# Reordering the joins of seven partial products on GpSimd, and one attention sum on VectorE, in a fused attention + MLP kernel

## The chip, the core and the metric

One Trainium2 chip, one of its cores. The metric is the device time of one execution in microseconds (us). The kernel before: median 1112.72 us of 3 runs (1112.7 to 1113.13).

## What is computed

The input is a 2048 x 576 matrix `x`. With `xn = layernorm(x)` the output is `x + A(xn) + B(xn)`:

```python
xn = _layernorm(x, axis=-1)
return x + _A_ref(xn, A_wqkv, A_wo) + _B_ref(xn, B_w1, B_b1, B_w2)
# A: 32 heads of 18; each position attends to itself and 7 earlier ones, 2 apart, then @ wo
# B: h = xn @ w1 + b1 (576 -> 4608); act = h * tanh(softplus(h)) (Mish); act @ w2 (4608 -> 576)
```

Everything is float32. The kernel splits each operand of a matrix product into a high part (a cast to fp32r) and a low part (operand minus high part), and adds three matmuls per product for it.

## The kernel before, in words

The 2048 rows are worked in two halves of 1024. For each half the kernel computes q, k, v (`qkv_item`), then the MLP in 18 steps of 256 hidden columns; behind the second half comes the output projection `wo` (`wo_part`). The attention itself never touches TensorE (PE): GpSimd (POOL) multiplies queries with windows of keys (`pr`, line 539) and weights with values (`pv`, line 577), VectorE (DVE) sums these products (lines 544 and 583) and ScalarE (ACT) takes the exponentials. This work runs beside the MLP, one piece per slot.

**Slots.** The order of all work is written out by hand. `plan` is a list of slots; each holds one piece of PE work (`add`), and `before(i, fn)` puts other work into slot `i` in front of the piece. Each engine then executes its own instructions strictly in the order in which this loop emits them. So a number in a `before` call decides what stands behind what on an engine's queue.

**The second half's MLP.** For its first 8 hidden steps the second product (`act @ w2`) is done by a scheme of seven products in place of eight (Strassen-like), `p_item` at line 861: `P7, P4, P1, P5, P2, P6, P3` in this order, for `e` = 0 to 3, each into its own accumulator `pacc[name, pr]` (two tiles of 128 x 576, `pr` = 0 and 1). Slot `("p","x",e,k)` is product `k` of round `e`. A product is 24 matmuls into four PSUM tiles `po` (line 872; the tag "out" has 4 buffers), and DVE adds each to the accumulator (line 878; ACT copies for P1, P6 and P7 in round 0, line 876). PE can begin the next user of a `po` buffer only once that addition is done.

**The joins.** When all rounds are done, `p_join(a, b, pr)` (line 880) adds one accumulator to another on POOL. There are seven for each `pr`: P6+=P1, P7+=P6, P6+=P5, P2+=P1, P3+=P6, P4+=P7, P5+=P7. The results P2, P3, P4, P5 are the four quarters of the output; `m2_cols` (line 884) then adds the remaining hidden steps to them: 24 matmuls a slot (line 893), four DVE additions (line 896), the slot for `pr` = 0 or 1 of the rows `b` = 1 first, into P4 and P5, later `b` = 0 into P2 and P3.

**Names and lines that the steps below touch.** `a_split` (lines 834, 835): ACT casts the high part of `act`, POOL subtracts for the low part. `u_high`, `u_low` (820, 826): the same for the operands of the seven products, the low part on POOL or DVE. `mish` (725, 726, 731, 732): DVE adds two PSUM parts, ACT takes Mish, ACT and POOL split. `take` (714): ACT copies a PSUM tile. Lines 680 and 686 are the matmuls of the MLP's first product, `h`.

**Where an attention sum stands.** `attention` issues a product on POOL and leaves its sum on DVE (line 544) to be flushed with the next piece. A set `behind_adds` holds slots in which the sum is emitted behind the slot's piece (and so behind its four additions on DVE); elsewhere it stands in front of them.

Of the kernel before, what the change touches and what calls it, by code (L numbers as in the profile page):

```python
# [31 lines left out]
OC = 4  # L32
# [7 lines left out]
def block_kernel(ctx: ExitStack, tc: tile.TileContext, x, wq, wo, w1, b1, w2, mask, out):  # L40
# [469 lines left out]
    behind_adds, behind_next, now = set(), set(), [0]  # L510
# [318 lines left out]
    def a_split(b, j):  # L829
        q = 2 * OC  # L830
        t = rawact[q, b, j]
        assert owner[where[q, b, j]] == (q, b, j) and (q, f"A{b + 1}{j + 1}") in held_
        a = acts[1, q, b, j] = sb.tile([P, 2, TB], F32R, tag=f"a{b}", bufs=(3, 2)[b], name=f"act_1_{b}_{2 * q + j}")
        nc.scalar.copy(a[:, 0, :], t)
        nc.gpsimd.tensor_tensor(out=a[:, 1, :], in0=t, in1=a[:, 0, :].bitcast(F32), op=ALU.subtract)
# [44 lines left out]
    def p_join(a, b, pr):  # L880
        nc.gpsimd.tensor_tensor(out=pacc[a, pr], in0=pacc[a, pr], in1=pacc[b, pr], op=ALU.add)
# [274 lines left out]
    at = {}  # L1156
# [7 lines left out]
    def before(i, fn):  # L1164
        plan[max(i, 0)][1].append(fn)
# [17 lines left out]
    items = []  # L1183
# [172 lines left out]
    def spot(hf, q, i):  # L1356
        return at["s", hf, q, i]

    for q in range(NP):
        if q == 0:  # L1360
            i = at["q", 0, 3, 1, 0]
            ps_ = dict(raw=i - 3, sums=i - 1, wa=i, wc=i + 1, t0=i + 2, t1=i + 4)
        elif q == 1:
            i = at["q", 0, 3, 0, 0]
# [16 lines left out]
    for q in range(1, 2 * OC + 1):  # L1381
        i = spot(0, q, (3,2)[q > 1])
# [5 lines left out]
    i = spot(0, NP - 1, 0)  # L1388
# [5 lines left out]
    i = at["q", 1, 0, 1, 1]  # L1394
# [4 lines left out]
    i = spot(0, 9, 4)  # L1399
# [10 lines left out]
    for q in range(NP):  # L1410
        if q == 0:
            i = at["z", JB - 1, 0]
            ps_ = dict(wa=i - 7, t0=i - 6, t1=i - 5, wc=i - 4)
        elif q == 1:
            i = spot(1, 0, 0)
# [22 lines left out]
    J = 2 * OC + 1  # L1438
    for b in range(NB):
        for j in range(2):  # L1440
            before(spot(1, J, 0) + (2,3,1,2)[2 * b + j], lambda b=b, j=j: a_split(b, j))
    for n, (a, b) in enumerate((("P6", "P1"), ("P7", "P6"), ("P6", "P5"), ("P2", "P1"), ("P3", "P6"), ("P4", "P7"), ("P5", "P7"))):
        for pr in range(2):
            i = items[-2][2] + 1 + (0,1,2)[n] if n < 3 else at["p", 1, J + 0 - 1, n > 4, pr] + (1, 7, 1, 2)[n - 3]
            before(i, lambda a=a, b=b, pr=pr: p_join(a, b, pr))

    i = at["q", 0, 1, 1, 0]
# [3 lines left out]
    i = at["q", 0, 3, 1, 0]  # L1451
# [5 lines left out]
    i = at["q", 1, 0, 1, 1]  # L1457
# [9 lines left out]
    for n in range(0, JB, 2):  # L1467
        i = at["q", 0, 1, 0, n]
# [4 lines left out]
    for n in range(TJ):  # L1473
        i = spot(0, 2 + n, 2)
# [3 lines left out]
    i = spot(0, NP - 2, 0)  # L1478
# [7 lines left out]
    for n, (name, pr) in enumerate((name, pr) for name in ("P4", "P5", "P2", "P3") for pr in range(2)):  # L1486
        i = items[dict(P4=0, P5=2, P3=2, P2=3)[name]][2] + pr
# [2 lines left out]


    att = {}
    behind_adds.update((at["p", "x", OC - 1, 4], at["p", "x", 0, 4]))
    behind_next.add(at["m", 1, 10, 3])
    T = [0.0]
    for p_ in plan:
# [37 lines left out]
    i = spot(1, *(11,3))  # L1534
# [11 lines left out]
    i = spot(1, NP - 1, 0)  # L1546
# [26 lines left out]
    last = {}  # L1573
# [44 lines left out]
```

## Time and profile before

| What | Value |
|---|---|
| Median of the runs shown | 1112.72 us |
| The profiled execution's own time | 1113.35 us |
| Its span, first to last instruction | 1111.6 us |
| PE busy | 1101.6 us, 99% of the span |
| DVE, POOL, ACT busy | 850.2, 789.8, 498.9 us |
| Granted TensorE clock | 1.000 |

The profile counts an engine as busy while an instruction of it is under way. A row of a timeline gives start, length, engine, line, operation and tiles, the number of merged instructions, and in brackets the idle time of that engine ahead of the row with what ended it. Merged rows overlap a little, as matmuls are pipelined: the distance between two rows' starts is the better measure of what a group costs. 1.75 us of the profiled execution lie outside its span (1113.35 - 1111.6).

### The profile page before, as it was taken

To read this page: it belongs to the slowest core of one execution; us is meant where nothing else is said; L and a number is where in the kernel's file an instruction comes from. 1 tells how busy PE (TensorE), PEld (TensorE's weight loads), DVE (VectorE), ACT (ScalarE), POOL (GpSimd) and SP (SyncE) were. 2 spreads that over 40 slices of the span, in tenths; PEclk is the share of its full clock that TensorE was granted. 3 is DMA by queue.
4 is the path that set the end of the run, shared out by engine and by line. 5 is a ranking of instruction groups with operands and counts; after the bars stand their busy time and mean duration, and the time that the engine had idled before them with its cause. 6 is when DMAs were issued, how large, how long until landed. Compare 5 with 4: busy or idle time off the path is not lost.

```text
span 1111.6 us, 18209 instructions
## 1 busy us (share of the span) xinstructions
PE 1101.6 (99%) x6550; PEld 1014.5 (91%) x6550; DVE 850.2 (76%) x1367; ACT 498.9 (45%) x917; POOL 789.8 (71%) x639
## 2 busy tenths in 40 slices
PE   8999999999999999999999999999999999999998
PEld 7999899999999999999999888999888999999998
DVE  6359788888889888897656567877876677777786
ACT  5544655544454544555333354443432344343353
POOL 2479777766779688685788666666688976867542
PEclk9999999999999999999999999999999999999999
DMA  6899696868777768675598799656674657776674
GB/s 200 284 311 312 231 346 225 282 237 274 255 247 263 264 212 298 249 255 201 187 322 268 225 378 304 214 189 207 219 230 161 210 195 214 245 284 219 183 233 142
DMA packets 178270, 271.60 MB, mean 244 GB/s; under 512 B 53218, under 2 KB 120068, under 8 KB 178180
## 3 DMA queue, kind: packets, MB, share of 16 engines
q1 hardware_dynamic: 178180, 270.44, 72.3%
q8 instruction: 52, 0.85, 0.3%
q14 instruction: 38, 0.31, 0.1%
HBM read 160.39 MB, written 110.00 MB: 243 GB/s over the span
## 4 chain that ended last, share of the span: by engine, by line
PE 90%; DMA 4%; DVE 2%; POOL 1%; ACT 1%; SPq 1%; issue 1%; POOLq 0%; DVEq 0%
PE h L680 27%; PE po L780 21%; PE pq L348 11%; PE po L893 11%; PE po L872 6%; PE h L686 5%; PE o L1076 5%; PE z L446 3%; DMA acc<-in_x 1%; DMA kv<-kv_d 1%; DMA t<-kept_t 1%; DMA accP<-in_x 1%; SPq L612 1%; POOL act L732 1%; DMA pw<-kept_T 1%
## 5 line engine op out<-in xcount | busy, mean ns | idle before, releaser
L780 PEld LDWEIGHTS po<-w,act 128*128 128x128 f32 x1728 | 236.4, 188 | 6.0 <-POOL act L732 0.4
L780 PE MATMUL po<-w,act 128*128 128x288 f32 x1728 | 240.7, 295 | 0.1
L539 POOL TENSOR_TENSOR pr<-q,kv 128x576 f32<-128x576 f32 x128 | 197.3, 1566 | 8.1 <-DMA q<-q_d 4.9
L732 POOL TENSOR_TENSOR act<-c,act 128x512 fp32r<-128x512 f32 x81 | 107.4, 1327 | 128.5 <-ACT act L731 127.9
L577 POOL TENSOR_TENSOR pv<-L,kv 128x576 f32<-128x576 f32 x128 | 178.4, 1488 | 24.8 <-DVE L L570 19.9
L784 DVE TENSOR_TENSOR acc<-po,acc 128x288 f32<-128x288 f32 x288 | 119.5, 449 | 29.9 <-PE po L780 28.8
L348 PE MATMUL pq<-wq,xt 128*128 128x432 f32 x672 | 136.4, 361 | 1.1 <-ACT xt L81 1.1
L893 PEld LDWEIGHTS po<-w,act 128*128 128x128 f32 x960 | 130.9, 188 | 5.9 <-DVE accP L896 3.0
L893 PE MATMUL po<-w,act 128*128 128x288 f32 x960 | 133.3, 295 | 2.4 <-DVE accP L896 2.4
L348 PEld LDWEIGHTS pq<-wq,xt 128*128 128x128 f32 x672 | 125.0, 188 | 8.1 <-ACT xt L81 1.9
L726 ACT ACTIVATE c<-c,b1c 128x512 f32<-128x512 f32 x81 | 58.7, 725 | 140.9 <-DVE c L725 140.6
L680 PE MATMUL h<-xt,t 128*128 128x512 f32 x432 | 110.6, 391 | 0.7 <-DVE rt L725 0.7
L680 PE MATMUL h<-S,t 128*128 128x512 f32 x432 | 110.5, 391 | 0.0
L583 DVE TENSOR_REDUCE og<-pv 128x144 f32<-128x1152 f32 x64 | 85.9, 1345 | 23.9 <-POOL pv L577 23.8
L680 PE MATMUL h<-xt,wa 128*128 128x512 f32 x432 | 104.1, 390 | 0.0
L544 DVE TENSOR_REDUCE L<-pr 128x64 f32<-128x1152 f32 x64 | 85.8, 1342 | 23.3 <-POOL pr L539 23.2
L714 ACT COPY c<-h 128x512 f32<-128x512 f32 x81 | 47.4, 586 | 124.5 <-PE h L686 73.4
L680 PEld LDWEIGHTS h<-xt,wa 128*128 128x128 f32 x432 | 80.9, 188 | 17.0
L872 PEld LDWEIGHTS po<-pw,u 128*128 128x128 f32 x672 | 91.9, 188 | 3.8 <-DVE accP L878 1.3
L872 PE MATMUL po<-pw,u 128*128 128x288 f32 x672 | 94.1, 295 | 0.5 <-DVE accP L878 0.3
L680 PEld LDWEIGHTS h<-xt,t 128*128 128x128 f32 x432 | 79.1, 188 | 15.6 <-DVE rt L725 1.2
L896 DVE TENSOR_TENSOR accP<-po,accP 128x288 f32<-128x288 f32 x160 | 69.0, 452 | 31.7 <-PE po L893 29.0
(228 smaller groups left out, 1852.1 us busy)
## 6 DMA issues: line engine op xcount, KB each, us to landing
kv<-kv_d SPq DMA_DIRECT2D x64, 396.0 KB, 4.8
kept_t<-t SPq DMA_DIRECT2D x36, 512.0 KB, 4.8
t<-kept_t SPq DMA_DIRECT2D x36, 512.0 KB, 6.4
rw<-in_w SPq DMA_DIRECT2D x36, 320.0 KB, 4.8
kept_wa<-wa SPq DMA_DIRECT2D x18, 640.0 KB, 4.9
kept_w<-w SPq DMA_DIRECT2D x20, 576.0 KB, 4.2
wa<-kept_wa SPq DMA_DIRECT2D x18, 640.0 KB, 5.2
w<-kept_w SPq DMA_DIRECT2D x20, 576.0 KB, 4.1
```

The source lines that it names most:

```text
L348: nc.tensor.matmul(pq[:, 0:432], XT[:, xi, tok], wt[wi][:, hl, 0:432], start=i == 0, stop=i == len(seq) - 1)
L539: nc.gpsimd.tensor_tensor(out=pr[:, x:x + hh], in0=q[:, j0 + x:j0 + x + hh, None, :].to_broadcast([P, hh, W, CU]), in1=win(kt, 0, CU, j0 + ...
L544: nc.vector.tensor_reduce(L[:, k, j0:j0 + hj].rearrange("p j w h -> p (j w h)"), pr.rearrange("p j w (h d) -> p (j w h) d", h=2), axis=AX, ...
L577: nc.gpsimd.tensor_tensor(out=pr[:, x:x + hj].rearrange("p j d w -> p j w d"), in0=L[:, k, x:x + hj, :, h:h + 1].to_broadcast([P, hj, W, DH]),
L583: nc.vector.tensor_reduce(og[:, c0:c0 + DH, :].rearrange("p d j -> p j d"), pr, axis=AX, op=ALU.add)
L680: nc.tensor.matmul(ph, wt[:, wl, wk * P:(wk + 1) * P], X[:, xs, :], start=first and i == 0, stop=last and i == len(seq) - 1, skip_group_ch ...
L732: nc.gpsimd.tensor_tensor(out=a[:, 1, :], in0=t, in1=a[:, 0, :].bitcast(F32), op=ALU.subtract)
L780: nc.tensor.matmul(po, acts[hf, q, b, j][:, al, tok], done["w2", hf, 2 * q + j][:, wl, c * HC:(c + 1) * HC], start=i == 0, stop=i == 5)
L784: nc.vector.tensor_tensor(out=t, in0=po, in1=t, op=ALU.add)
L872: nc.tensor.matmul(po, units[e, k, qq][:, al, tok], w[:, qq, wl, :], start=i == 0, stop=i == 5)
L893: nc.tensor.matmul(po, acts[hf, q, b, j][:, al, tok], done["w2", hf, 2 * q + j][:, wl, c * HC:(c + 1) * HC], start=i == 0, stop=i == 5)
L896: nc.vector.tensor_tensor(out=t, in0=po, in1=t, op=ALU.add)
```

## The change

The seven joins become another seven with the same four results. P6+=P5 followed by P3+=P6 is replaced: P5 is now added to P3 itself, in the slot of the last round's P6 product (`last`), three slots before P6+=P5 stood, and P3+=P6 later brings only P6 and P1. P7+=P6 moves one slot later. P6+=P1 and the four later joins keep their slots. Apart from that, one slot leaves `behind_adds`: that of product P2 in round 0, whose attention sum now stands in front of the four additions.

```diff
-    for n, (a, b) in enumerate((("P6", "P1"), ("P7", "P6"), ("P6", "P5"), ("P2", "P1"), ("P3", "P6"), ("P4", "P7"), ("P5", "P7"))):
-        for pr in range(2):
-            i = items[-2][2] + 1 + (0,1,2)[n] if n < 3 else at["p", 1, J + 0 - 1, n > 4, pr] + (1, 7, 1, 2)[n - 3]
+    last = at["p", "x", OC - 1, 5]
+    for pr in range(2):
+        for a, b, i in (("P3", "P5", last), ("P6", "P1", last + 1), ("P7", "P6", last + 3),
+                        ("P2", "P1", at["p", 1, J - 1, 0, pr] + 1), ("P3", "P6", at["p", 1, J - 1, 0, pr] + 7),
+                        ("P4", "P7", at["p", 1, J - 1, 1, pr] + 1), ("P5", "P7", at["p", 1, J - 1, 1, pr] + 2)):
             before(i, lambda a=a, b=b, pr=pr: p_join(a, b, pr))
...
-    behind_adds.update((at["p", "x", OC - 1, 4], at["p", "x", 0, 4]))
+    behind_adds.add(at["p", "x", OC - 1, 4])
```

What moves on the engines. First POOL, at the end of the seven products (`accP6_0` is the accumulator P6 for `pr` = 0, `act_1_1_16` a low part that `m2_cols` multiplies, `pr_1_3_0_1` an attention product). Before:

```order
L835 TENSOR_TENSOR act_1_1_16_9257<-rm2_7261,act_1_1_16_9257 128x512
L881 TENSOR_TENSOR accP6_0_7863<-accP6_0_7863,accP1_0_7480 128x576
L881 TENSOR_TENSOR accP6_1_7880<-accP6_1_7880,accP1_1_7658 128x576
L835 TENSOR_TENSOR act_1_0_16_9282<-ra2_7257,act_1_0_16_9282 128x512
L835 TENSOR_TENSOR act_1_1_17_9285<-rt0_7264,act_1_1_17_9285 128x512
L881 TENSOR_TENSOR accP7_0_7529<-accP7_0_7529,accP6_0_7863 128x576
L881 TENSOR_TENSOR accP7_1_7546<-accP7_1_7546,accP6_1_7880 128x576
L539 TENSOR_TENSOR pr_1_3_0_1_9291<-q_1_6_8854,kv0_1_6_8852 128x576 x2
L732 TENSOR_TENSOR act_1_0_20_9298<-c11_1_9_9269,act_1_0_20_9298 128x512
L835 TENSOR_TENSOR act_1_0_17_9333<-rm1_7260,act_1_0_17_9333 128x512
L881 TENSOR_TENSOR accP6_0_7863<-accP6_0_7863,accP5_0_7476 128x576
L881 TENSOR_TENSOR accP6_1_7880<-accP6_1_7880,accP5_1_7477 128x576
```

The same place of the changed kernel:

```order
L881 TENSOR_TENSOR accP3_0_7478<-accP3_0_7478,accP5_0_7476 128x576
L881 TENSOR_TENSOR accP3_1_7479<-accP3_1_7479,accP5_1_7477 128x576
L835 TENSOR_TENSOR act_1_1_16_9259<-rm2_7261,act_1_1_16_9259 128x512
L881 TENSOR_TENSOR accP6_0_7863<-accP6_0_7863,accP1_0_7480 128x576
L881 TENSOR_TENSOR accP6_1_7880<-accP6_1_7880,accP1_1_7658 128x576
L835 TENSOR_TENSOR act_1_0_16_9284<-ra2_7257,act_1_0_16_9284 128x512
L835 TENSOR_TENSOR act_1_1_17_9287<-rt0_7264,act_1_1_17_9287 128x512
L539 TENSOR_TENSOR pr_1_3_0_1_9291<-q_1_6_8854,kv0_1_6_8852 128x576 x2
L732 TENSOR_TENSOR act_1_0_20_9298<-c11_1_9_9271,act_1_0_20_9298 128x512
L835 TENSOR_TENSOR act_1_0_17_9333<-rm1_7260,act_1_0_17_9333 128x512
L881 TENSOR_TENSOR accP7_0_7529<-accP7_0_7529,accP6_0_7863 128x576
L881 TENSOR_TENSOR accP7_1_7546<-accP7_1_7546,accP6_1_7880 128x576
```

The pair that reads P5 went from the end of these rows to their front, and the P7 pair from ahead of the attention product to the end: the product now has two joins fewer ahead of it since the last `act` split, and none of the twelve rows is new or gone.

Then DVE in round 0 (`accP2` is the accumulator of product P2, `L_1_1` the attention sums, `u_0_6_1` an operand's low part). Before:

```order
L814 TENSOR_TENSOR rm4_7263<-rm4_7263,rm3_7262 128x512
L878 TENSOR_TENSOR accP2_0_7472<-po_0_4_0_0_7811,accP2_0_7472 128x288
L878 TENSOR_TENSOR accP2_0_7472<-po_0_4_0_1_7819,accP2_0_7472 128x288
L878 TENSOR_TENSOR accP2_1_7473<-po_0_4_1_0_7827,accP2_1_7473 128x288
L878 TENSOR_TENSOR accP2_1_7473<-po_0_4_1_1_7835,accP2_1_7473 128x288
L544 TENSOR_REDUCE L_1_1_7745<-pr_1_1_0_0_7747 128x64
L826 TENSOR_TENSOR u_0_6_1_7846<-rm4_7263,u_0_6_1_7846 128x512
L814 TENSOR_TENSOR rm0_7259<-ra2_7257,rm0_7259 128x512
L725 TENSOR_TENSOR rt1_7265<-h3_1_3_7777,rt1_7265 128x512
```

The same place of the changed kernel:

```order
L814 TENSOR_TENSOR rm4_7263<-rm4_7263,rm3_7262 128x512
L544 TENSOR_REDUCE L_1_1_7745<-pr_1_1_0_0_7747 128x64
L878 TENSOR_TENSOR accP2_0_7472<-po_0_4_0_0_7812,accP2_0_7472 128x288
L878 TENSOR_TENSOR accP2_0_7472<-po_0_4_0_1_7820,accP2_0_7472 128x288
L878 TENSOR_TENSOR accP2_1_7473<-po_0_4_1_0_7828,accP2_1_7473 128x288
L878 TENSOR_TENSOR accP2_1_7473<-po_0_4_1_1_7836,accP2_1_7473 128x288
L826 TENSOR_TENSOR u_0_6_1_7846<-rm4_7263,u_0_6_1_7846 128x512
L814 TENSOR_TENSOR rm0_7259<-ra2_7257,rm0_7259 128x512
L725 TENSOR_TENSOR rt1_7265<-h3_1_3_7777,rt1_7265 128x512
```

The sum moved past four additions; everything from the `u` row on keeps its place. PE, ACT and the DMA queue have the same rows in the same order in both kernels.

## The prediction

> **What bounds the kernel now.** I read the page first. PE is busy for 99% of the span, so a change is worth what it takes from, or adds to, the few places where PE stands still; time saved on another engine counts only if PE waits for it.
>
> ```profile
> PE 1101.6 (99%) x6550; PEld 1014.5 (91%) x6550; DVE 850.2 (76%) x1367; ACT 498.9 (45%) x917; POOL 789.8 (71%) x639
> ```
>
> Next the list of what PE waited for from 640 us to the end (total, times, longest):
>
> ```profile
> PE po L893 <- DVE accP L896: 2.4, 2, 1.7
> PE h L680 <- DVE rt L725: 0.7, 1, 0.7
> PE po L872 <- DVE accP L878: 0.3, 1, 0.3
> ```
>
> The largest wait is on line 893, behind DVE's additions to the join's results; the two small ones are those beside the attention sum that moves. So the change touches just the places where PE is idle. Behind them PE has no gap at all (busy time of PE, PEld, DVE, ACT, POOL, then the clock, in one stretch):
>
> ```profile
> 840.00:1054.00 214.00, 214.00 (x1322) 197.41 (x1321) 157.56 (x257) 82.14 (x124) 162.22 (x124) 1.00 0.65 220
> ```
>
> PE is busy for 214.00 of 214.00 us at clock 1.00, while POOL has 52 us free and DVE 56. What PE gains before 840 it should therefore carry to the end.
>
> PE around the big wait, in order of time:
>
> ```profile
> 830.21 1.53 PE L680 MATMUL h<-S,t 128*128 128x512 f32 x6
> 831.58 0.61 PE L686 MATMUL h<-xt,wc 128*128 128x512 f32 x2
> 833.85 1.85 PE L893 MATMUL po<-w,act 128*128 128x288 f32 x12 [1.66 <-DVE accP L896]
> 836.43 1.86 PE L893 MATMUL po<-w,act 128*128 128x288 f32 x12 [0.73 <-DVE accP L896]
> 838.13 1.54 PE L680 MATMUL h<-xt,t 128*128 128x512 f32 x6
> ```
>
> There are two waits in one group of 24 matmuls. DVE explains each:
>
> ```profile
> 832.08 1.35 DVE L544 TENSOR_REDUCE L<-pr 128x64 f32<-128x1152 f32 x1 [7.11 <-POOL pr L539]
> 833.35 0.81 DVE L896 TENSOR_TENSOR accP<-po,accP 128x288 f32<-128x288 f32 x2
> 835.91 0.82 DVE L896 TENSOR_TENSOR accP<-po,accP 128x288 f32<-128x288 f32 x2 [1.75 <-POOL accP L881]
> ```
>
> DVE had nothing it could do for 7.11 us: its next instruction in order was an attention sum whose product POOL had not made. The additions that free PE's four `po` buffers stood behind it. Then the third addition, the first into P5, waited 1.75 us more for a join on POOL: P6+=P5 reads P5, so P5 may not be overwritten before. POOL itself:
>
> ```profile
> 818.92 1.29 POOL L835 TENSOR_TENSOR act<-rm,act 128x512 fp32r<-128x512 f32 x1 [3.67 <-ACT act L834]
> ...
> 825.21 1.29 POOL L835 TENSOR_TENSOR act<-rt,act 128x512 fp32r<-128x512 f32 x1 [0.52 <-ACT act L834]
> 826.46 2.83 POOL L881 TENSOR_TENSOR accP<-accP,accP 128x576 f32<-128x576 f32 x2
> 829.23 2.81 POOL L539 TENSOR_TENSOR pr<-q,kv 128x576 f32<-128x576 f32 x2
> 832.00 1.27 POOL L732 TENSOR_TENSOR act<-c,act 128x512 fp32r<-128x512 f32 x1
> 833.23 1.28 POOL L835 TENSOR_TENSOR act<-rm,act 128x512 fp32r<-128x512 f32 x1
> 834.46 2.79 POOL L881 TENSOR_TENSOR accP<-accP,accP 128x576 f32<-128x576 f32 x2
> ```
>
> From 826.46 POOL is without a gap: P7+=P6, the attention product, two low parts, P6+=P5. Just before, it stood idle for 3.67 us.
>
> **Part 1: the joins.** Nothing is added or removed, four instructions move. (a) P3+=P5 stands where the 3.67 us gap is, 815.25 to 818.92, and needs 2.8 us (two joins, as at 826.46). P5 has had its last addition by then. P3 has not: DVE's additions of the last product now wait for this join, but PE begins that product only at 821.14 (its row stands with the rivals). The join ends at about 818.1, before POOL's next work can begin at 818.92: cost nothing, hidden by the wait for ACT's cast; without that gap it would cost POOL 2.8 us, of which the 0.52 us gap at 825.21 takes back a part. (b) P7+=P6 leaves 826.46, so the attention product runs 826.46 to 829.25 and its sum on DVE starts at about 829.3 instead of 832.08. Its first addition then starts at 829.3 + 1.27 (833.35 - 832.08) = 830.6 and frees a buffer at about 831.0. (c) The wait of 1.75 us goes altogether, since P5 was read at 818. What is late next? PE's own matmuls: the four buffers are full at 830.2, where line 680 begins, line 686 follows, and the next group can start 0.46 us after 831.58 (the distance of 686 to the following group in the rows of part 2), at 832.04. A buffer is free since 831.0, so PE does not wait. Without waits the group takes 3.17 us, and the work that started at 838.13 starts at 832.04 + 3.17 = 835.21: **2.92 us earlier**. The idle rows alone give 1.66 + 0.73 = 2.39 us; the other 0.5 us are what restarting the pipeline twice costs. Those are the bounds of this term, 2.4 and 2.9, and I take the upper, as it comes from starts that are measured.
>
> (d) P7+=P6 now runs where P6+=P5 ran, behind the two low parts (1.27 and 1.28 us), which come 2.8 us earlier. POOL's queue behind it is 2.8 us earlier too, about what PE gains, so every later low part keeps its lead over PE to a tenth. P4+=P7, the first to use P7, stands behind the next attention product and nobody waits for it. SP's queue is untouched.
>
> **Part 2: the attention sum in front of its additions.** DVE and PE in round 0:
>
> ```profile
> 684.99 1.54 DVE L878 TENSOR_TENSOR accP<-po,accP 128x288 f32<-128x288 f32 x4
> 686.45 1.34 DVE L544 TENSOR_REDUCE L<-pr 128x64 f32<-128x1152 f32 x1
> 687.71 0.68 DVE L826 TENSOR_TENSOR u<-rm,u 128x512 fp32r<-128x512 f32 x1
> 688.31 0.68 DVE L814 TENSOR_TENSOR rm<-ra,rm 128x512 f32<-128x512 f32 x1
> 688.91 0.68 DVE L725 TENSOR_TENSOR rt<-h,rt 128x512 f32<-128x512 f32 x1
> ```
>
> ```profile
> 685.49 3.44 PE L872 MATMUL po<-pw,u 128*128 128x288 f32 x24 [0.30 <-DVE accP L878]
> 689.65 1.66 PE L680 MATMUL h<-xt,t 128*128 128x512 f32 x6 [0.71 <-DVE rt L725]
> 691.14 0.62 PE L686 MATMUL h<-xt,wa 128*128 128x512 f32 x2
> 691.60 3.33 PE L872 MATMUL po<-pw,u 128*128 128x288 f32 x24
> 694.77 1.53 PE L680 MATMUL h<-S,wc 128*128 128x512 f32 x6
> 696.13 0.62 PE L686 MATMUL h<-xt,wc 128*128 128x512 f32 x2
> ```
>
> PE's group of 685.49 starts when the first addition is done. The sum now goes first and takes 687.71 - 686.45 = 1.26 us of DVE, so the group starts at 686.75. It lasts 3.17 us (691.60 to 694.77) plus 0.11 for the restart (3.44 against 3.33): it ends at 690.03. PE then used to wait for DVE's line 725 until 689.65. Line 725 stands behind all five instructions in either order and ends as before, so this wait of 0.71 us swallows most of the delay: 690.03 - 689.65 = 0.38 us stay, less the restart that goes with the wait (691.14 - 689.65 = 1.49 against 1.36 from 694.77 to 696.13), so **0.25 us later**. Bounds: 0, if the wait takes all, and 1.26, if line 725 moves with it. A gain I exclude: the sum frees a POOL buffer earlier, but POOL's next instruction waited for ACT, not for it:
>
> ```profile
> 692.13 1.29 POOL L826 TENSOR_TENSOR u<-rm,u 128x512 fp32r<-128x512 f32 x1 [4.39 <-ACT u L820]
> ```
>
> **Sum.** -2.92 + 0.25 = -2.67 us. The profiled execution, 1113.35 us (span 1111.6 and 1.75 around it), would become 1110.7; it is 0.63 above the median of the runs, 1112.72, for which I say 1110.1. A measurement of this kernel tells about 0.2% from no change, 2.2 us, so the line is at 1110.5 and the forecast lies only 0.4 us beyond it.
>
> **Rivals.** *The full price of the sum.* If line 725 moves with the additions, 1.26 us stay: 1112.72 - 2.92 + 1.26 = 1111.1. For it speaks that DVE is tight there; against it that its five instructions need the same time in any order.
>
> *No price for it:* 1109.8.
>
> *The transfer holds the product.* In the chain of work that ended last these two pieces follow each other:
>
> ```profile
> 826.26 4.33 DMA kv<-kv_d
> ...
> 830.61 1.43 POOL pr L539
> ```
>
> If the load landing at 830.59 releases the product's second half, moving joins away from ahead of it does nothing, the first wait stays and only the second goes: PE starts at 833.85, does 24 matmuls in 3.28, and gets to 837.13 in place of 838.13; 1112.72 - 1.0 + 0.25 = 1112.0. Against it: the two halves start 1.38 us apart, as POOL's back-to-back halves do, and the product reads the keys of head 6, while the load of 826.26 brings values that are used later. Releasers are inferred, and here by coincidence.
>
> *The join ahead holds up DVE.* DVE's operations from SBUF to SBUF stretch next to POOL's:
>
> ```profile
> 817.42 0.65 DVE L826 TENSOR_TENSOR u<-rm,u 128x512 fp32r<-128x512 f32 x1
> 817.99 1.54 DVE L878 TENSOR_TENSOR accP<-po,accP 128x288 f32<-128x288 f32 x4
> 819.45 1.31 DVE L826 TENSOR_TENSOR u<-ra,u 128x512 fp32r<-128x512 f32 x1
> ```
>
> With POOL idle it took 0.65 us, next to POOL 1.31. P3+=P5 now lies on the first one, until 818.1, so it ends 0.7 later, and so do four additions. The second then is issued at 820.1, but it had waited for POOL's instruction of 818.92 until 820.2 in any case and ends at 820.8 as before. So I charge nothing. If it were pushed by a whole 1.3 us, to 822.1, it would be late for the third matmul of the last product, which PE begins here:
>
> ```profile
> 821.14 3.33 PE L872 MATMUL po<-pw,u 128*128 128x288 f32 x24
> ```
>
> That is less than 0.9 us: 1111.0. The Trainium skill, page "SBUF — State Buffer", section "Who interferes with whom", says that a VectorE instruction with two SBUF inputs and a GpSimd instruction that reads SBUF exclude each other, whoever issues first holding on for its whole length. By that rule it is the first L826 that blocks, as reckoned here, and the sum stays.
>
> *Slower.* The sum in front makes P2's additions hang on POOL's product in round 0. That is made from 676.21 to 679.04, 5.9 us before the sum's turn at 684.99:
>
> ```profile
> 676.21 2.83 POOL L539 TENSOR_TENSOR pr<-q,kv 128x576 f32<-128x576 f32 x2
> ```
>
> ```profile
> DMA to landing us min/median/max: 1.7/2.1/9.1
> ```
>
> POOL comes to it behind two differences that wait for loads into `accP`, whose landing times spread by 7 us. If the product is later by more than 5.9 us, each further us goes to the additions and to PE one for one. From 8.6 us on this eats the whole gain (5.9 plus 2.67), and at 11 us the kernel ends at 1112.72 - 2.67 + 5.1 = 1115.1. The spread seen does not reach that.
>
> *The change does not do what it says*, the gain being given back behind 840: POOL is the tightest there, 162 of 214 us; about 1112.5.
>
> **How the numbers follow.** Forecast 1110.1, 0.56, with its own range 1109.6 to 1110.6: 0.46 of it below 1110.5. No price 0.09 (faster). Full price 0.13, transfer 0.09, join ahead 0.05, given back 0.04, all within 0.2%, but for 0.01 slower of the last; slower by the late product 0.04. So faster 0.55, same 0.40, slower 0.05. The range reaches over the full price and the transfer, 1109.3 to 1112.1, and leaves out the late product and the gain given back.
>
> **What would show it.** Right: in the changed profile PE's wait on line 893 is gone from the list; DVE's 7.11 us ahead of line 544 is about 4.3; no DVE addition of line 896 waits for line 881; POOL's 3.67 us gap has shrunk to about 0.8; in round 0 PE's wait for line 878 is about 1.5 us and that for line 725 is gone. Wrong: a wait of about 1.7 us left on line 893 (the transfer), a wait on line 725 left beside the longer one on 878 (full price), a new wait of PE for line 826 near 821, or any gap of PE behind 840.

## The result, and the profile after

The changed kernel takes **1110.03 us** (median of 12 executions, 1109.51 to 1110.49), the kernel before 1112.97 us in the same session (12 executions): a ratio of 0.9972, 95% interval 0.9964 to 0.9981. That is 2.94 us faster; the forecast was 1110.1 us, and 2.67 us of gain. The profiled execution took 1110.25 us, its span is 1108.5 us.

The list of what PE waited for from 640 us to the end had three rows before. Now it has one (total, times, longest):

```profile
PE po L872 <- DVE accP L878: 0.9, 1, 0.9
```

The waits on line 893 are gone, and so is the one for line 725. PE around the place of the big wait:

```profile
831.40 0.62 PE L686 MATMUL h<-xt,wc 128*128 128x512 f32 x2
831.85 3.34 PE L893 MATMUL po<-w,act 128*128 128x288 f32 x24
835.03 1.53 PE L680 MATMUL h<-xt,t 128*128 128x512 f32 x6
```

From line 686 to the next line 680 PE took 838.13 - 831.58 = 6.55 us before; it takes 835.03 - 831.40 = 3.63 us now. The difference is 2.92 us. The rest of the change of the span (3.1 us, from 1111.6 to 1108.5) is that PE arrived 0.18 us earlier in this execution.

DVE and POOL at that place:

```profile
829.12 1.35 DVE L544 TENSOR_REDUCE L<-pr 128x64 f32<-128x1152 f32 x1 [4.33 <-POOL pr L539]
830.39 1.54 DVE L896 TENSOR_TENSOR accP<-po,accP 128x288 f32<-128x288 f32 x4
```

```profile
815.10 2.82 POOL L881 TENSOR_TENSOR accP<-accP,accP 128x576 f32<-128x576 f32 x2
818.72 1.30 POOL L835 TENSOR_TENSOR act<-rm,act 128x512 fp32r<-128x512 f32 x1 [0.80 <-ACT act L834]
...
826.27 2.81 POOL L539 TENSOR_TENSOR pr<-q,kv 128x576 f32<-128x576 f32 x2
...
834.32 2.85 POOL L539 TENSOR_TENSOR pr<-q,kv 128x576 f32<-128x576 f32 x2
```

The first pair of joins lies in what was a gap of 3.67 us, of which 0.80 is left. The attention product starts at 826.27, DVE's idle time ahead of its sum is 4.33 instead of 7.11 us, and the four additions follow it as one row, with no wait for a join between them. Behind that PE has no gap:

```profile
838.00:1051.00 213.00, 213.00 (x1315) 196.41 (x1314) 156.77 (x258) 82.13 (x124) 161.41 (x123) 1.00 0.65 221
```

PE in round 0, where the sum now stands in front of the additions:

```profile
684.77 0.61 PE L686 MATMUL h<-xt,wc 128*128 128x512 f32 x2
686.30 3.44 PE L872 MATMUL po<-pw,u 128*128 128x288 f32 x24 [0.92 <-DVE accP L878]
689.58 1.54 PE L680 MATMUL h<-xt,t 128*128 128x512 f32 x6
690.96 0.61 PE L686 MATMUL h<-xt,wa 128*128 128x512 f32 x2
```

### The profile page after: what moved, and what is told of

The parts are those of the page before. It is cut to its first block, busy times and chain, and to the rows that moved or that the text cites. A ratio compares the mean times of both kernels' runs of the same rounds, so it can differ in the third digit from the quotient of the medians.

```text
span 1108.5 us, 18208 instructions
## 1 busy us (share of the span) xinstructions
PE 1100.6 (99%) x6550; PEld 1014.4 (92%) x6550; DVE 851.2 (77%) x1367; ACT 499.1 (45%) x917; POOL 789.4 (71%) x639
## 4 chain that ended last, share of the span: by engine, by line
PE 94%; DMA 2%; DVE 1%; ACT 1%; POOL 1%; issue 1%; SPq 0%; DVEq 0%; POOLq 0%
PE h L680 29%; PE po L780 21%; PE po L893 11%; PE pq L348 11%; PE po L872 7%; PE h L686 6%; PE o L1076 5%; PE z L446 4%; DMA acc<-in_x 1%; DMA accP<-in_x 1%; POOL act L732 0%; PE ta L75 0%; DVE rm L814 0%; DVE og L583 0%; ACT u L820 0%
```

## The experiments

Each was compared with runs of the kernel before on the same chip; over all of these and the 12 above the kernel before has a median of 1113.06 us (97 executions). "The joins alone" below means the changed kernel's joins with the sum left behind its additions.

**The full change once more.** No edit.

> The changed kernel once more, as the measure for its parts on the same chip. Theory (joins give 2.92 us, the attention sum in front takes back 0.25): 2.7 us below the kernel before, about 1110.1. Rival (the sum in front costs its full 1.26 us and the joins give more than reckoned): the same here; only the parts tell them apart.

Measured: 1110.36 us, ratio 0.9986 (0.9973 to 0.9999). Eight of the 11 executions lie between 1109.57 and 1110.94; in the other three, 1112.64 to 1116.24, the granted clock was 0.996 to 0.998 instead of 1.000. With the 12 of the result the median of 23 executions is 1110.12.

**The joins alone**, in two kernels that are the same, in different sessions:

```diff
-    behind_adds.add(at["p", "x", OC - 1, 4])
+    behind_adds.update((at["p", "x", OC - 1, 4], at["p", "x", 0, 4]))
```

> Only the joins are changed, the attention sum stands behind its additions as before. Theory: PE's stretch from 831.6 to 838.1 is 2.92 us shorter and round 0 is as before, so 2.9 us below the kernel before and 0.25 below the full change (about 1109.9). Rival, full price of the sum: 1.3 below the full change (1108.8). Rival, the sum in front gains something: above the full change.

> The joins of the changed kernel alone, the sum where it was before: a second measurement beside the kernel with the later sum. Theory: the sum in front costs 0.25 us, so this is 0.25 us below the full change's 1110.03, at 1109.8. Rival: the sum in front costs nothing, 1110.03, or all of its 1.26 us, 1108.8.

Measured: 1109.68 us (5 executions), ratio 0.997 (0.9958 to 0.9982), and 1110.1 us (7), ratio 0.9973 (0.9962 to 0.9983); together a median of 1110.07. The joins bring all of the gain: 1113.06 - 1110.07 = 2.99 us. In the time of whole executions the sum's place makes no difference that shows: 1110.07 without it, 1110.12 with it.

**The sum alone.** The kernel before, with the same line as in the full change:

```diff
-    behind_adds.update((at["p", "x", OC - 1, 4], at["p", "x", 0, 4]))
+    behind_adds.add(at["p", "x", OC - 1, 4])
```

> Only the attention sum of round 0 goes in front of its four additions. Theory: PE's wait for line 878 there grows from 0.3 to about 1.5 us, its wait for line 725 goes, and the kernel is 0.25 us slower than before (about 1113.2), within noise. Rival, full price: 1.26 slower (1114.2), with the wait for line 725 still there. Rival, a gain: below 1112.8.

Measured: 1113.1 us (11 executions), ratio 0.9999 (0.9991 to 1.0008). The time cannot tell 0.25 us from nothing, but the traces can, once the right starting point is found. DVE's row of instructions in round 0 does not begin with PE. Followed back, it begins with POOL's second difference of line 858, which waits for a load of `x`. Of the kernel before:

```profile
673.58 1.42 POOL L858 TENSOR_TENSOR accP<-accP,accP 128x576 f32<-128x576 f32 x1 [1.49 <-DMA accP<-in_x]
```

The same difference of the sum alone, and where PE got to:

```profile
672.60 1.44 POOL L858 TENSOR_TENSOR accP<-accP,accP 128x576 f32<-128x576 f32 x1 [1.50 <-DMA accP<-in_x]
```

```profile
685.79 3.46 PE L872 MATMUL po<-pw,u 128*128 128x288 f32 x24 [0.84 <-DVE accP L878]
690.46 0.62 PE L686 MATMUL h<-xt,wa 128*128 128x512 f32 x2
```

From that difference to PE's line 686 at the end of the round, in seven profiles:

| Kernel | Second difference | PE's line 686 | Distance, us |
|---|---|---|---|
| before (sum behind) | 673.58 | 691.14 | 17.56 |
| joins alone, second (sum behind) | 673.45 | 691.03 | 17.58 |
| changed (sum in front) | 673.12 | 690.96 | 17.84 |
| changed, once more (sum in front) | 672.76 | 690.61 | 17.85 |
| sum alone (sum in front) | 672.60 | 690.46 | 17.86 |
| two sums in front, below | 672.82 | 690.65 | 17.83 |
| sum behind line 725, below | 673.26 | 690.71 | 17.45 |

The six other profiles with the sum behind its additions give 17.56 to 17.59. So the sum in front costs 17.84 - 17.57 = **0.27 us**, in four profiles out of four. The second difference starts up to 0.98 us earlier or later from one profile to the next (672.60 to 673.58), and PE follows it. Among such shifts whole times don't show 0.27.

**P3+=P5 alone.** The joins alone, with P7+=P6 back in its old slot:

```diff
-("P7", "P6", last + 3)
+("P7", "P6", last + 2)
```

> P5 is added to P3 in the slot ahead in place of P6, but P7+=P6 keeps its old slot in front of the attention product; the sum as before. Theory: the wait for a late attention product stays (PE starts its group about 1.8 us late), the second wait, for the join that reads P5, goes: 1.0 us below the kernel before (about 1112.0). Rival, the read of P5 was the whole obstacle: 2.9 below. Rival, a transfer holds the product: also 1.0 below, and no different from the full joins.

Measured: nine of 12 executions between 1111.28 and 1112.34 (their median is 1111.75), median of all 1111.85; the other three, at 1117.68 to 1118.83, had a clock of 0.997 to 0.998. Ratio 1.0002 (0.9987 to 1.0016) over all. PE:

```profile
831.54 0.61 PE L686 MATMUL h<-xt,wc 128*128 128x512 f32 x2
833.81 3.45 PE L893 MATMUL po<-w,act 128*128 128x288 f32 x24 [1.66 <-DVE accP L896]
837.10 1.54 PE L680 MATMUL h<-xt,t 128*128 128x512 f32 x6
```

The first wait stays and the second goes: 837.10 - 831.54 = 5.56 us instead of 6.55. That is 1.0 us at the place, as reckoned for the case in which the product is not made earlier; in time the nine executions are 1.3 us below the kernel before.

**P7+=P6 alone.** The kernel before, with P7+=P6 moved into the slot of P6+=P5, ahead of it:

```diff
-            i = items[-2][2] + 1 + (0,1,2)[n] if n < 3 else ...
+            i = items[-2][2] + 1 + (0,2,2)[n] if n < 3 else ...
```

> P6+=P5 and its target stay; only P7+=P6 goes one slot later, behind the attention product (and directly ahead of P6+=P5). The sum as before. Theory: the attention product and its sum come 2.8 us earlier and PE starts its group without a wait, but the addition into P5 still waits until P6+=P5 has read it, at the same time as before, so PE is held there instead: 0 us, between 0.2 faster and 0.2 slower (about 1113.0). Rival, the two waits add up: 1.9 us below the kernel before, what the full joins give less the 1.0 of the second wait.

Measured: 1114.12 us (11 executions, 1112.43 to 1116.46), ratio 1.001 (1.0001 to 1.002).

```profile
831.14 1.74 PE L893 MATMUL po<-w,act 128*128 128x288 f32 x12
835.54 2.46 PE L893 MATMUL po<-w,act 128*128 128x288 f32 x12 [2.66 <-DVE accP L896]
837.80 2.53 PE L680 MATMUL h<-xt,t 128*128 128x512 f32 x6
840.17 0.62 PE L686 MATMUL h<-xt,wa 128*128 128x512 f32 x2
```

The first wait goes, but the second takes over all of it, since P6+=P5 stands where it stood and the third addition needs it: one wait of 2.66 us in place of 1.66 and 0.73. So the two moves don't add up; either alone brings 1.0 us or nothing, both together 2.9. There is more. The matmuls behind the wait are slow: 12 of them take 2.26 us to the next row, against 838.13 - 836.43 = 1.70 before, and the six of line 680 2.37 against 1.4. The windows show why (columns as before, the clock is the third number from the end):

```profile
835.50:836.50 1.00, 0.96 (x7) 0.96 (x8) 1.00 (x3) 0.02 (x1) 1.00 (x2) 1.00 0.00 0
836.50:839.90 3.40, 3.40 (x12) 2.97 (x11) 2.24 (x5) 1.32 (x2) 3.40 (x3) 0.50 0.00 0
839.90:850.00 10.10, 10.10 (x66) 9.40 (x65) 5.48 (x11) 2.66 (x4) 10.10 (x9) 1.00 0.05 13
```

One us after PE resumed its clock was halved for 3.4 us, which costs about 1.7 us. In eight of the 11 executions the mean clock was 0.997 or 0.998, and these took 1113.65 to 1116.46 us; in the three at 1.000 they took 1112.43 to 1113.12, the time of the kernel before.

**The idle time made longer.** The kernel of the last experiment, with a third pair of joins ahead of P6+=P5 in the same slot (P7 here takes in P1 once too often, and with it the outputs P4 and P5). Against the kernel before:

```diff
-(("P6", "P1"), ("P7", "P6"), ("P6", "P5"), ("P2", "P1"), ...
+(("P6", "P1"), ("P7", "P6"), ("P7", "P1"), ("P6", "P5"), ("P2", "P1"), ...
...
-            i = items[-2][2] + 1 + (0,1,2)[n] if n < 3 else ...
+            i = items[-2][2] + 1 + (0,2,2,2)[n] if n < 4 else ...
```

> The kernel with P7+=P6 beside P6+=P5 in one slot, and a third pair of joins between them, P7+=P1, 2.8 us on POOL (P1 is added to P7 once too often, and so to the outputs P4 and P5). PE's idle time on line 893 grows from 2.66 to about 5.4 us. Theory, the clock goes down when an idle time is long enough: with 2.66 us it went down in 8 of 11 executions, with 5.4 us it goes down in all; low for about 3.4 us, which costs 1.7. Time: 1112.8 (the three executions of 2.66 us with the clock at 1.000) + 2.8 + 1.7 = 1117.3. Rival, the clock's drops have nothing to do with the length of the idle time: some executions stay at 1.000, and their time is 1115.6.

Measured: 1118.64 us (4 executions, 1118.25 to 1120.38), ratio 1.0053 (1.004 to 1.0067), and the clock at 0.997 in each of the four. PE's wait is 5.37 us. PE, then two windows of its profile:

```profile
838.90 3.25 PE L893 MATMUL po<-w,act 128*128 128x288 f32 x12 [5.37 <-DVE accP L896]
```

```profile
833.60:837.30 3.70, 0.00 (x0) 0.00 (x0) 0.00 (x0) 0.00 (x0) 3.70 (x4) 1.00 0.15 60
837.30:844.10 6.80, 5.20 (x18) 4.71 (x19) 4.32 (x8) 1.34 (x2) 6.80 (x6) 0.51 0.00 0
```

The clock is low for 6.8 us, twice the 3.4 of before, and PE works in 5.2 of them, which costs 2.6 us rather than the 1.7 expected: 1112.8 + 2.7 + 2.6 = 1118.1, half a us below the measured time. The theory's direction stands, the length of the low stretch was mis-sized.

**The same slot, the pairs swapped.** P7+=P6 in the slot of P6+=P5 again, but behind it (P7 takes in P5 as well, and so do P4 and P5). Against the kernel before:

```diff
-(("P6", "P1"), ("P7", "P6"), ("P6", "P5"), ("P2", "P1"), ...
+(("P6", "P1"), ("P6", "P5"), ("P7", "P6"), ("P2", "P1"), ...
...
-            i = items[-2][2] + 1 + (0,1,2)[n] if n < 3 else ...
+            i = items[-2][2] + 1 + (0,2,2)[n] if n < 3 else ...
```

> The kernel with P7+=P6 beside P6+=P5 in one slot, but with the two pairs swapped: P6+=P5 comes first. (P7 takes in P5 as well here, and so do the outputs P4 and P5.) Theory: what held PE for 2.66 us was only that P6+=P5 stood behind two other joins on POOL. First in the slot, its half for tile 0 ends at about 832.2, and DVE's third addition is wanted at 832.9: PE's waits on line 893 are gone, the clock stays at 1.000 in all executions, and the time is that of the full change, about 1110.1. Rival: any join after the attention product makes the additions wait, whichever comes first; then 1.3 us or more of the wait stay: 1111.5 to 1114.

Measured: 1112.4 us (10 executions, 1111.71 to 1113.77), ratio 0.9994 (0.9985 to 1.0003). The theory was half right. The wait at 832 is gone and the clock is 1.000 in all ten, but most of the gain is given back a little later (in time 0.6 us of it is left):

```profile
831.79 3.54 PE L893 MATMUL po<-w,act 128*128 128x288 f32 x24
835.18 1.53 PE L680 MATMUL h<-xt,t 128*128 128x512 f32 x6
...
841.55 0.61 PE L686 MATMUL h<-xt,wc 128*128 128x512 f32 x2
842.30 3.44 PE L893 MATMUL po<-w,act 128*128 128x288 f32 x24
...
850.76 3.18 PE L893 MATMUL po<-w,act 128*128 128x288 f32 x22 [0.19 <-POOL act L732]
...
856.03 3.44 PE L893 MATMUL po<-w,act 128*128 128x288 f32 x24 [0.71 <-DVE accP L896]
```

```profile
837.04 2.86 POOL L539 TENSOR_TENSOR pr<-q,kv 128x576 f32<-128x576 f32 x2
```

Two pairs of joins stand ahead of it, from 831.49 on (four instructions, 5.63 us), and so POOL's next product starts at 837.04 instead of 834.32, 2.7 us later than in the changed kernel, while PE is as early. PE is then held up three times between 841 and 856: the group of 842.30 starts 0.75 us behind line 686 instead of 0.45, and the rows of 850.76 and 856.03 name POOL's low part and DVE's additions as what they waited for. By line 680 behind the group of 866.31 it is 869.48 - 867.35 = 2.1 us behind the changed kernel, though it left 835 only 0.15 us later. So the order alone does not bring the gain; a pair of joins has to leave this stretch, as it does in the change for the gap at 815.

**Without the gap.** The joins alone, with P3+=P5 one slot later, where POOL has no gap:

```diff
-("P3", "P5", last)
+("P3", "P5", last + 1)
```

> The joins as changed, but P3+=P5 one slot later, behind the first low part, so that POOL's idle time ahead of it no longer covers it. The sum as before. Theory: POOL's queue is 2.8 us longer where it counts; the low part act of line 835 comes late for PE by about 1.1 us and the attention product by 2.4, so PE's group starts 1.4 us later than with the full joins: 1.5 us below the kernel before. Rival, the gap is of no importance as long as P5 is read early: 2.9 below.

Measured: 1111.63 us (11 executions, 1110.71 to 1112.58), ratio 0.9989 (0.998 to 0.9998): 1.6 us above the joins alone.

```profile
818.49 1.30 POOL L835 TENSOR_TENSOR act<-rm,act 128x512 fp32r<-128x512 f32 x1 [3.58 <-ACT act L834]
819.74 6.06 POOL L881 TENSOR_TENSOR accP<-accP,accP 128x576 f32<-128x576 f32 x4
```

```profile
828.32 2.79 PE L893 MATMUL po<-w,act 128*128 128x288 f32 x19 [0.88 <-POOL act L835]
```

The gap of 3.6 us stands empty again, and P3+=P5, now the first two of four joins in a row, holds up the low part of line 835 that follows them (from 825.76; 823.20 in the changed kernel), for which PE waits 0.88 us. The gap is what makes P3+=P5 free.

**Two sums in front.** The changed kernel without the last slot of `behind_adds`:

```diff
-    behind_adds.add(at["p", "x", OC - 1, 4])
```

> The full change, and the attention sum beside product P2 of the last round goes in front of its additions as well. Theory: DVE's additions come 1.26 us later, the first is done 0.8 us after PE wants its buffer, and here no later wait of PE takes this up: 0.9 us above the full change (1110.9). Rival, DVE's idle 4.3 us a little later take it up: as the full change (1110.0). Rival, the whole of the sum's time: 1.3 above.

Measured: 1110.98 us (11 executions, 1110.48 to 1111.55), ratio 0.9981 (0.9972 to 0.9989): 0.9 us above the changed kernel. Round 3, DVE and PE:

```profile
813.45 1.34 DVE L583 TENSOR_REDUCE og<-pv 128x144 f32<-128x1152 f32 x1
814.72 1.53 DVE L878 TENSOR_TENSOR accP<-po,accP 128x288 f32<-128x288 f32 x4
```

```profile
815.26 3.41 PE L872 MATMUL po<-pw,u 128*128 128x288 f32 x24 [0.76 <-ACT u L820]
```

The additions start 1.3 us later, behind the sum, and the group waits 0.76 us plus its restart. Nothing behind swallows it, as line 725 does in round 0. The trace names ACT's cast as the releaser, because that ended last, at 815.20. In the changed kernel the same cast ended at 815.45, when the group had been running for 0.9 us, so the first matmuls don't need it; the `po` buffers are left.

**The sum later still.** The joins alone, with the sum of round 0 behind line 725:

```diff
-                    plan[now[0] + 1][0].append(behind[0])
+                    plan[now[0] + 1 + (now[0] == at["p", "x", 0, 4])][0].append(behind[0])
...
-    behind_next.add(at["m", 1, 10, 3])
+    behind_next.update((at["m", 1, 10, 3], at["p", "x", 0, 4]))
```

> All joins of the changed kernel, and the sum of round 0's P2 slot later still: behind DVE's addition of line 725 for which PE waited 0.71 us when the sum stood behind the four additions. Theory: line 725 ends 1.26 us earlier, so PE's next matmuls of line 680 follow the group of 24 without a wait: 0.71 us of wait and 0.13 to 0.2 of restart are won, the wait for line 878 stays as short as with the sum behind (0.3 to 0.4). Time 0.85 us below the joins alone: about 1108.9. Rival: DVE makes up nothing, because line 826 and the next sum behind it come later for somebody; then as the joins alone, 1109.7, with a new wait of PE near 691 to 695 us.

Measured: 1109.99 us (8 executions, 1109.6 to 1110.75), ratio 0.9973 (0.9963 to 0.9984): as the joins alone, 1110.07. The time is the rival's, but no new wait of PE appears; the mechanism is neither's. DVE, first in the second kernel of the joins alone, then here:

```profile
686.34 1.33 DVE L544 TENSOR_REDUCE L<-pr 128x64 f32<-128x1152 f32 x1
687.60 0.68 DVE L826 TENSOR_TENSOR u<-rm,u 128x512 fp32r<-128x512 f32 x1
688.80 0.68 DVE L725 TENSOR_TENSOR rt<-h,rt 128x512 f32<-128x512 f32 x1
```

```profile
686.16 1.83 DVE L826 TENSOR_TENSOR u<-rm,u 128x512 fp32r<-128x512 f32 x1
688.51 0.68 DVE L725 TENSOR_TENSOR rt<-h,rt 128x512 f32<-128x512 f32 x1
```

Line 826 takes 1.83 us instead of 0.68. POOL's product beside it ends at 687.43, and 0.56 us later the subtraction is done:

```profile
684.18 3.25 POOL L539 TENSOR_TENSOR pr<-q,kv 128x576 f32<-128x576 f32 x2
```

The sum had stood in the time in which POOL's product would have stretched that subtraction. Taken away, it won 1.26 us and lost 1.15. The Trainium skill, page "SBUF — State Buffer", section "Who interferes with whom", has the port pair that DVE's second input and GpSimd share as an exclusive lock; the subtraction has two inputs in SBUF, the sum has one and kept its 1.33 beside the same product, so the rows agree with it.

**The load earlier.** The last three experiments left the load of `x` as what starts round 0. The joins alone, with the loads into P3 one slot earlier:

```diff
-        before(i - (1 if name == "P3" else 2), lambda name=name, pr=pr: x_send(name, pr))
+        before(i - (2 if name == "P3" else 2), lambda name=name, pr=pr: x_send(name, pr))
```

> The changed kernel's joins, the sum where it was before, and the two loads of x into P3 issued one slot earlier: the second one then stands ahead of a load of 512 KB and one of 288 KB in the DMA queue. Theory: round 0 is late because POOL's second difference of line 858 waits about 1.5 us for that load (1.49 us in the profiles of the kernel before and of the joins alone); at some 390 GB/s the 800 KB less ahead of it bring it in 2.05 us earlier, so this wait goes, DVE's chain up to line 725 comes 1.49 us earlier, and PE's waits of 0.3 us for line 878 and of 0.7 us for line 725 vanish with their restarts. PE reaches the end of round 0 1.5 us earlier, and the time is 1108.6 against 1110.07 for the joins alone. Rival: PE's place there is set by its own matmuls or by the loads pushed back by 288 KB, 0.74 us each; then the time stays at 1110 or is up to 0.7 us above, and a new wait of PE or of a cast appears between 668 and 690 us.

Measured: **1108.85 us** (5 executions, 1108.51 to 1109.18), ratio 0.9959 (0.9945 to 0.9973), which is 1.2 us under the joins alone and the changed kernel. These ran in other sessions; against the kernel before in its own session, 1113.39 us there, this kernel gains 4.54 us, 1.55 more than the joins alone. POOL and PE:

```profile
670.42 2.86 POOL L858 TENSOR_TENSOR accP<-accP,accP 128x576 f32<-128x576 f32 x2
```

```profile
684.43 0.62 PE L686 MATMUL h<-xt,wc 128*128 128x512 f32 x2
684.88 3.33 PE L872 MATMUL po<-pw,u 128*128 128x288 f32 x24
688.05 1.54 PE L680 MATMUL h<-xt,t 128*128 128x512 f32 x6
689.43 0.61 PE L686 MATMUL h<-xt,wa 128*128 128x512 f32 x2
```

The two differences follow each other without a wait, PE goes from row to row, and from 640 to 1060 us its list of waits is empty. From 684.43 to 689.43 PE took 5.00 us; before it took 691.14 - 684.57 = 6.57. The profile shows 1.57 us where 1.49 was expected, the times 1.2 to 1.55.

## Why the prediction was right

**The joins.** The term was -2.92 us, between 2.4 and 2.9. The profile after shows 2.92 at the place, the joins alone 2.99 in time. The steps behind it hold one by one: the product without two joins ahead of it (826.27 instead of 829.23), the sum's wait of 4.33 us, no wait for a join, and PE's own matmuls as what is late next. The upper bound was the right one to take, since a wait costs the restart too, not only its idle row. That both moves are needed was shown by doing each alone: 1.0 us and nothing.

**The time.** That 1110.03 us lies within 0.1 us of the forecast is in part luck. The forecast was taken off 1112.72 us, the median of three executions, and the kernel before took 1112.97 in the session of the result. The gain was forecast as 2.67 and measured as 2.94 us, with an interval of 2.1 to 4.0, so the 0.3 us between them cannot be told from noise. The two terms hold by the traces, not by the time.

**That POOL's queue behind is earlier as well** was one sentence of the prediction, and it turned out to carry 2.1 us. Swapping the pairs took the wait away just as well, but left POOL as late as in the kernel before, and PE caught up with it. The rival "the gain is given back" therefore has a mechanism in this kernel; the change escapes it because a pair of joins moves into the gap. Its cover was tested too: without the gap, 1.6 us are lost.

**The sum in front.** The term was +0.25 us, and the traces show 0.27, measured from the instruction that starts the row. Full price (1.26) and a gain are excluded; in the time alone it would have stayed unsettled. But one number of this step failed: PE's wait for line 878 was said to become about 1.5 us, and it was 0.92, 1.30, 0.84 and 0.76 in the four profiles with the sum in front. The prediction took the distance between PE and DVE in round 0 from one execution as fixed. DVE's row hangs on the landing of a load, and the difference behind that load moves by up to 0.98 us between profiles, while what is late last, line 725, moves with it. The price didn't depend on that, the wait did.

**The rivals.** The transfer does not hold the product: it starts at 826.27 and its sum follows it at 829.12. The join ahead does stretch DVE's first subtraction, and it costs nothing, as reckoned, since the second would have waited for POOL anyway. The rows of the changed kernel:

```profile
817.29 1.18 DVE L826 TENSOR_TENSOR u<-rm,u 128x512 fp32r<-128x512 f32 x1
819.85 0.71 DVE L826 TENSOR_TENSOR u<-ra,u 128x512 fp32r<-128x512 f32 x1
```

1.18 and 0.71 us in place of 0.65 and 1.31: the long one is now the first, and the second ends at 820.56 instead of 820.76. The late product (the slower case) did not come: the difference that waits for the load moved by 1 us, well below the 5.9 us of slack. The spread of 7 us on which this case was built is a misreading. The row of 1.7 to 9.1 us takes all transfers of `accP` together, with the 16 that write the output; the eight loads of `x` alone took 7.2 to 9.1 us to land in the profile before, a spread of 1.9. No run made the product later on purpose, so the price of that case is only argued.

**What the prediction did not see** is why round 0 waits at all. It stopped at line 725 and took its end as given. Further back on the same row stands the wait of 1.49 us for a load, which it used for a rival and never as the cause of PE's idle time. Moving that load is worth 1.2 to 1.55 us.

## What to carry to other kernels

When a wait goes, ask what feeds the same engines 10 to 20 us later: an early PE runs into a late POOL, and a move into an idle gap of POOL is worth more than the same move in a full stretch. Price a small reordering from the instruction that starts its row, not from an engine that happens to be near, and follow that row back until it reaches a load or an engine without a gap. Two waits in one group can share one cause or take each other's place, so do each part alone before adding up their rows.

## What the runs showed of the hardware

- **The clock falls after an idle time of PE shorter than the stretch for which it then stays low.** With 2.66 us between matmuls (2.90 between weight loads) the mean clock was 0.997 or 0.998 in eight of 11 executions, and in the profiled one it was halved for 3.4 us; with 5.37 us it was 0.997 in four of four, and in the profiled one halved for 6.8 us. With the pairs swapped, and no such wait, it stayed at 1.000 in ten of ten. A wait of 1.66 us, alone or with one of 0.73 behind it, left it at 1.000 in the profiles. The Trainium skill, page "TensorE: Matmul & The Clock Gate", section "What's actually happening", gives a free-running window of about 3.4 us and half rate after at least one idle window. The length of the low stretch and the chance in it agree with a free-running window; that it takes a whole idle window does not, by the 2.66 us here, and the measurement decides. Which share of a window has to be idle was not tried.
- **A two-input subtraction of DVE next to a POOL product took 1.83 us instead of 0.68**, while a sum with one input kept its 1.33. So a sum in front of a subtraction can be worth as much as it costs.
- **The clock also fell in kernels whose profiles show no wait of PE above 1.7 us**: to 0.996 to 0.998 in three of 11 executions of the full change's repeat and three of 12 of P3+=P5 alone. Seven of the 85 executions of the kernel before beside the experiments show 0.998 or 0.999. No profile caught one of these, so where it fell, and why, stays open.
